# Eight of the first front's norms on GpSimd, the second power table's pools released tile by tile, all orders written anew

## The chip, the cores and the metric

The kernel runs on one core of one Trainium2 chip. The metric is the device time of a whole execution in microseconds (us). Three runs of the kernel before took 402.38, 403.27 and 403.44 us, median 403.27. PE is TensorE, PEld its weight load, DVE VectorE, ACT ScalarE, POOL GpSimd and SP SyncE; "L1108" is line 1108 of the kernel before.

## The reference

Four residual layers on `x` (1 x 2048 x 512, bf16): sliding attention A, state-space convolution B, and both again with the same weights. In A each of 32 heads (16 elements each) looks at 8 positions, two apart. B's convolution kernel `K` is a sum over 128 complex states, the same in both layers.

```python
def _A_ref(x, wqkv, wo):
    H = 32; Dh = D // H
    W, dil = 8, 2
    qkv = (x @ wqkv).reshape(B, S, 3, H, Dh).transpose(2, 0, 3, 1, 4)
    q, k, v = qkv[0], qkv[1], qkv[2]
    idx = pos[:, None] - (jnp.arange(W) * dil)[None, :]
    mask = idx >= 0
    logits = jnp.einsum("bhsd,bhswd->bhsw", q, k[:, :, idx_c, :]) * Dh ** -0.5
    attn = softmax(jnp.where(mask, logits, -1e9))
    o = jnp.einsum("bhsw,bhswd->bhsd", attn, v[:, :, idx_c, :])
    return o.transpose(0, 2, 1, 3).reshape(B, S, D) @ wo

def _B_ref(u, A_re, A_im, B_re, B_im, C_re, C_im, log_dt, Dskip):
    dt = jnp.exp(log_dt)[:, None]
    P = jnp.exp((dt * A)[:, :, None] * l[None, None, :])
    K = jnp.einsum("dn,dnl,dn->dl", Cc, P, dt * Bc).real
    y = irfft(rfft(pad(u, 2 * L)) * rfft(pad(K, 2 * L)))[:L]
    return y + u * Dskip

x = x + _A_ref(_layernorm(x), A_wqkv, A_wo)
x = x + _B_ref(_layernorm(x), A_re, A_im, B_re, B_im, C_re, C_im, log_dt, Dskip)
x = x + _A_ref(_layernorm(x), A_wqkv, A_wo)
x = x + _B_ref(_layernorm(x), A_re, A_im, B_re, B_im, C_re, C_im, log_dt, Dskip)
```

## The kernel before

`x` is held as 16 row tiles of 128 x 512, taken in four blocks of four. The kernel has five stages, and in each of them every engine takes its instructions in the order in which the program issues them; no scheduler reorders them. That order is written out by hand: a string with a letter or a word for each piece of work. The table gives the strings and roughly when the stage runs in the profiled execution.

| stage | string | us |
|---|---|---|
| first front, together with the making of `K` | `ORDERK`, read by `k_gen` (L995) | 0 to 110 |
| first attention core | `CORE0`, read by `LayerA.core` | 105 to 190 |
| first convolution and second front | `ORDER0`, `ORDERF` | 190 to 270 |
| second attention core | `CORE1` | 265 to 350 |
| second convolution | `ORDER1` | 350 to 401 |

*The first front and `K` (`ORDERK`).* `K` needs powers of a complex number for each channel and state. Eleven squarings make the powers with exponents 1, 2, 4 and so on: `s` squares on ACT (L1083), `i` is a doubled product and a difference on DVE (L1087, L1090). `b` copies each power into a table on ACT: `B_t` (L1099) or, for the powers from 8 to 128, `pow_t` (L1097), whose negated plane is another ACT copy (L1102) and whose repeated plane a DMA (`c`, L1105). `M` fills up `B_t` with products on DVE (L1108, through the scratch tile `cm_t`), seven groups, the last ones with the powers 256, 512 and 1024 as factors. `T` and `U` fill the second kind of table, `A_t`, in four chunks of 32: chunks 0 and 2 are `T` and stand in the pool `kg_tab0`, chunks 1 and 3 are `U` and stand in `kg_tab1`. `H` makes the heads of chunks 1 to 3 (L1225, an ACT copy). The first `H` calls `stage_two` (L1213), which closes the scratch pool `kg_small` and opens `kg_tab1` and `kg_out` on its room; these two wait until the whole of the old pool is released. `p` multiplies the tables on PE (L1266), `x` copies the products to `kgs` on ACT (L1274), and after the last letter `kgs` is stored (L1288). `G` are the steps that make the constant tables of the convolution: the mask products on POOL (L696) and, last of their kind, the store `w`.

Between these letters stands the first front. The layer norm of a row tile needs its sum and its sum of squares. For blocks 0 to 2 they are `a`, two passes on ACT for each row tile (L143, L1152); for block 3 `3`, one `bn_stats` on DVE. `l` are the small DVE operations that make the mean and the offset `ln_nb` (L1166, L1167, L1178), `W` makes the reciprocal deviation on ACT (L1184, L1185). `y` applies the norms of blocks 0 to 2, 12 on ACT (L193), and `z` those of block 3, 4 on DVE (L195). `t` transposes a block in two halves of eight 128 x 128 transposes (L1194), `e` copies each half to `xnT` on ACT (L1197), `k` and `q` project (L1204), `K` and `Q` copy the projections on ACT (L1209). `X` are the first three products of queries and keys (L340, `A_pr`, which take the room of `A_t` in `kg_tab0`), `Z` their sums on PE.

*The attention cores.* `m` multiplies queries and keys on DVE (L340), `l` sums on PE, `x`, `e`, `r`, `n` and `T` are the softmax. `P` multiplies weights and values on DVE (`pav`, L465), and `S` (half-width, L490) or `V` (whole-width, L480) sums on PE. `O` projects back and adds to `x`. `a` and `f` apply the norm of a row tile for the next layer on DVE and ACT. The core before the first convolution also holds the letters `A` to `H`, eight copies that bring `K` into `k_perm` (L1448); `KROWS` names the engine of each. `k_perm` and `g_i` also serve as scratch for an angle reduction on POOL (L728).

*The convolutions.* The transform of length 4096 is made of two steps. `K` and `U` are the first step for `K` and for the input, whose results are copied from PSUM into `a1s` (L788); `k` and `u` the second step, with copies to `kf_sb` and `ub` (L865); `m` is the product of the two spectra on DVE (L849, L852); `y` and `Y` are the first step of the inverse (half-width and whole-width on PE) with a copy to `z`; `z`, `w` and `v` the last step for different widths of columns, which adds to `x`. The second letter of a word names the engine of the copy or the addition: `A` is ACT, `D` is DVE.

*The second front (`ORDERF`).* `h` are the statistics of half rows, four `bn_stats` of 256 elements; `H` the same with whole rows of 512; `a` joins them; `p` makes the reciprocal deviation on ACT; `n` applies the norm of four row tiles, with `G` two on POOL and two on DVE and with `D` all four on DVE; `T` transposes, `E` copies the transposes, `P` and `Q` project.

Of the kernel before, what the change touches and what calls it, by code (L numbers as in the profile page):

```python
# [11 lines left out]
ALU = mybir.AluOpType  # L12
# [9 lines left out]
S = 2048  # L22
D = 512
H = 32
DH = 16
W = 8
NA = 16
NDT = 4
# [24 lines left out]
KD KA KA KA KD KA KD KA KD KA KD kA kD kA kA kD UA KD UA UD kA UA kD UA KD UA  # L53
UD UA KD kA u UD m UA KA u UD u UD m KA u kA m m UA u u kD m m u
UA u UD kA m UA kD kA u m kA kD u kA yA m YD m u m u YA u u m u
yA m m u yA m m YA yA yD yD
# [8 lines left out]
UA UD UA UD UA UA UD UA UD UA UD u UD u u UA m u m u m UA m u m u  # L65
UD m m UA u m u m u u yA YA u m m u yD m YA m u u m m u yA
YA m yA YD w000D yA yA yD yA z03D yA w010D yA yD yA z02D v103A v113D v112D v102D v110D v100A v111D v101A
"""

CORE0 = """  # L70
vvmvvlvmvvmlvxlemvrmnlqmqvlTvqlxevqmlvmvmPvvP1rnllxS0qTmqOeVmrqP4qSl2OPPSOSOPSmPP5On3l8ml6SPCOOV
AlxSPP7eOSrObSPn9POSdOESOPSPbDadBPfaGOtFOaaawVfHSbatO
"""
CORE1 = """
0m1l2ml3mvvqqlmmlmvqqvvllxmemqvlrnvvlmxTqqlvvmqlmvPvvvvmvqlleqVPrmxqmnqSTOePlPmSOPllSPOSPrOSnOPS
mOSPOblxOSPPdeOSrffbVPdfwOnPfVOPSOSPafbOPSdafftOSafatO
# [914 lines left out]
CH = 32  # L991
# [3 lines left out]
def k_gen(tc, nc, a_consts, ins, kd, la, x_v, lnst, zero, b_consts):  # L995

    B_L = (0, 1, 2, 3, 4, 5, 6, 7, 256, 258, 260, 262, 512, 516, 768, 772, 1024, 1280, 1536, 1792, 2048)
    NCH = P // CH
    with ExitStack() as ctx:
# [92 lines left out]
        def planes(k):  # L1092
            return cur[k][:].rearrange("p r (c x) -> p r c x", c=NCH)

        def power(k):
            if 3 <= k <= 7:
                nc.scalar.copy(Pw[:, :, k - 3, 1::2, :].rearrange("p c r x -> p r c x"), planes(k))  # L1097
            else:
                nc.scalar.copy(Bt[:, :, :, B_L.index(1 << k), :], cur[k][:].rearrange("p r (q g) -> p r q g", g=4))  # L1099

        def power_neg(k):
            nc.scalar.mul(Pw[:, :, k - 3, 2, :], planes(k)[:, 1], -1.0)  # L1102

        def power_copy(k):
            nc.sync.dma_start(Pw[:, :, k, 0, :], Pw[:, :, k, 1, :])  # L1105
# [48 lines left out]
        def norms():  # L1154
            D2 = D * D
            for b in range(4):
                cs = slice(4 * b, 4 * b + 4)
                rstd = la.fp.tile([P, 4], F32, name="ln_rstd")
                nb = la.fp.tile([P, 4], F32, name="ln_nb")
                ln[b] = rstd, nb  # L1160
                if b < 3:
                    mean, ms = lnst["s1"][:, cs], -1.0 / D
                    msq = la.fp.tile([P, 4], F32, name="ln_msq")
                    veps = la.fp.tile([P, 4], F32, name="ln_veps")
                    lvar[b] = veps[:]
                    yield lambda: nc.vector.scalar_tensor_tensor(msq[:], mean, -1.0 / D2, mean, ALU.mult, ALU.mult)  # L1166
                    yield lambda: nc.vector.scalar_tensor_tensor(veps[:], lnst["s2"][:, cs], 1.0 / D, msq[:], ALU.mult, ALU.add)  # L1167
                else:
                    ag = la.fp.tile([P, 4, 2], F32, name="ln_ag")
                    lvar[b] = ag[:, :, 1]  # L1170

                    def aggr():
                        for a in range(4):
                            nc.vector.bn_aggr(ag[:, a, :], lnst["bn"][:, 12 + a, 0, :])

                    yield aggr
                    mean, ms = ag[:, :, 0], -1.0
                yield lambda: nc.vector.scalar_tensor_tensor(nb[:], mean, ms, rstd[:], ALU.mult, ALU.mult)  # L1178
# [15 lines left out]
                    nc.tensor.transpose(pt[:, di, a, :], xb[b][:, a, (2 * d + di) * P:(2 * d + di + 1) * P], ident[:])  # L1194

        def turned(b, d):
            nc.scalar.copy(la.xnT[:, 2 * d:2 * d + 2, b * 512:(b + 1) * 512], xps[b, d][:].rearrange("p t a q -> p t (a q)"))  # L1197

        def proj(kind, b, ft, h):
            if h == 0:  # L1200
# [5 lines left out]

        def projected(kind, b, ft):
            dst = la.kT[:, ft, 14 + b * 4:18 + b * 4, :] if kind == "k" else la.qT[b][:, ft]
            nc.scalar.copy(dst.rearrange("p a q -> p (a q)"), pps[kind, b, ft][:])  # L1209
# [60 lines left out]
        def produced(c, q8):  # L1270
            if (c, q8) == (0, 0):
                late["kgs"] = late["kgp"].tile([P, NB * 4, P], BF16, name="kgs")
            q0 = c * CH + q8 * 8
            nc.scalar.copy(late["kgs"][:, :, q0:q0 + 8].rearrange("p m (h j) -> p m h j", h=2),  # L1274
                           pks[c, q8][:, :, 0:4 * NB * 4].rearrange("p h (j m) -> p m h j", j=4))

        def k_store():
# [44 lines left out]
        ops = dict(  # L1322
            s=calls(square, *((k,) for k in range(11))), i=[f for k in range(11) for f in calls(double, (k,)) + calls(differ, (k,))],
            b=[f for k in range(12) for f in calls(power, (k,)) + (calls(power_neg, (k,)) if 3 <= k <= 7 else [])],
            C=c_part(), M=b_part(), G=steps, w=[w2_store], c=calls(power_copy, *((k,) for k in range(5))),
            a=calls(pass_stats, *((b, a, i) for b in range(3) for a in range(4) for i in range(2))), l=norms(),
            W=calls(inv_std, *((b,) for b in range(4))), y=calls(apply, *((b, a, "act") for b in range(3) for a in range(4))),
            z=calls(apply, *((3, a, "dve") for a in range(4))),
            t=calls(turn, *((b, d) for b in range(4) for d in range(2))), e=calls(turned, *((b, d) for b in range(4) for d in range(2))),
            k=calls(proj, *(("k", b, ft, h) for b in range(4) for ft in fts for h in range(2))),  # L1330
            q=calls(proj, *(("q", b, ft, h) for b in range(2) for ft in fts for h in range(2))),
# [6 lines left out]
        ops["3"] = calls(lambda a: row_stats(nc, lnst, xb[3][:, a, :], 12 + a, "dve"), *((a,) for a in range(4)))  # L1338
# [240 lines left out]
```

## Time and profile before

The profiled execution took 402.72 us, 400.8 us of which is the span from its first to its last instruction; the median of the runs shown is 403.27. The granted TensorE clock was 0.999 of full speed. The table gives the busy time of each engine in seven stretches of the span, in us.

| stretch | PE | DVE | ACT | POOL |
|---|---|---|---|---|
| 0 to 10 | 3.16 | 6.15 | 7.37 | 9.17 |
| 10 to 100 | 44.30 | 89.27 | 82.35 | 12.46 |
| 100 to 180 | 73.25 | 79.77 | 57.81 | 32.06 |
| 180 to 270 | 81.55 | 83.16 | 80.85 | 11.43 |
| 270 to 350 | 76.59 | 79.08 | 56.18 | 1.02 |
| 350 to 380 | 25.29 | 28.41 | 28.51 | 0.00 |
| 380 to 400.8 | 15.88 | 15.65 | 12.94 | 0.00 |
| whole span | 320.0 | 381.5 | 326.0 | 66.1 |

A line of the groups reads: line of the code, engine, operation, output and inputs by the program's names, their shapes (partitions x elements) and types, the count; then the busy time of all, the mean of one in ns, and the idle time of the engine just before these instructions with what ended most of it. A line of the timeline gives the start of a run of like instructions, the time that they took together, the engine, the line and the operation; in brackets stands how long it waited and for what.

### The profile page before, as it was taken

What the parts mean: (1) busy time and instruction counts of PE and PEld (TensorE: products, weight loads), DVE (VectorE), ACT (ScalarE), POOL (GpSimd) and SP (SyncE); (2) the same over time, 40 slices, a digit from 0 to 9 for tenths busy, and PEclk for the clock granted to TensorE, in tenths of its full rate; (3) what the DMA queues carried; (4) which work ended last, traced back from release to release, by engine and by line L of the source; (5) the groups of instructions that cost most, each with busy time, mean ns of one, the idle gap of its engine ahead of it and who ended that gap; (6) DMA issues with size and microseconds to landing.
All of it is one profiled execution on the core that took longest, in us unless ns stands there. A gap on an engine that the chain in (4) does not pass through costs nothing.

```text
span 400.8 us, 14761 instructions
## 1 busy us (share of the span) xinstructions
PE 320.0 (80%) x6479; PEld 227.6 (57%) x6527; DVE 381.5 (95%) x475; ACT 326.0 (81%) x565; POOL 66.1 (17%) x79
## 2 busy tenths in 40 slices
PE   3000178789999899889997889999999998998795
PEld 2000037557635567656887878643456766667785
DVE  6999999999999999999999999979999999989995
ACT  7999999786656499888999998864655788989983
POOL 9402500000299600030500002300000001000000
PEclk9999999999999999999999999999999999999999
DMA  7942820323014855285235677740063009504606
GB/s 220 395 132 31 87 65 12 83 54 94 12 39 110 216 180 152 79 296 225 101 115 206 223 270 215 263 136 2 2 169 94 3 20 404 162 2 108 213 11 205
DMA packets 62322, 54.17 MB, mean 135 GB/s; under 512 B 33869, under 2 KB 50738, under 8 KB 60978
## 3 DMA queue, kind: packets, MB, share of 16 engines
q1 hardware_dynamic: 62250, 53.22, 43.6%
q8 instruction: 51, 0.84, 0.9%
q14 instruction: 13, 0.11, 0.1%
q10 hardware_dynamic: 8, 0.00, 0.0%
HBM read 30.15 MB, written 13.24 MB: 108 GB/s over the span
## 4 chain that ended last, share of the span: by engine, by line
PE 29%; DVE 21%; issue 9%; ACT 7%; DMA 4%; SPq 1%; POOL 0%; DVEq 0%; ACTq 0%
DVE pav L465 5%; PE pq L396 5%; PE pq L501 4%; PE po L490 4%; DVE prod L340 3%; PE pq L221 3%; DVE t L849 3%; DVE t L852 3%; DVE ln_bn L148 2%; PE pb L799 2%; DMA v_ext<-v_ext 2%; PE L L352 2%; DVE a1s L788 1%; PE pb L806 1%; PE pb L883 1%
## 5 line engine op out<-in xcount | busy, mean ns | idle before, releaser
L465 DVE TENSOR_TENSOR pav<-attn,v_ext 128x4096 bf16<-128x4096 bf16 (+1 forms) x34 | 72.6, 2169 | 0.2
L340 DVE TENSOR_TENSOR prod<-qT,kT_ext 128x4096 bf16<-128x4096 bf16 x29 | 66.6, 2322 | 0.4 <-ACT qT L223 0.3
L1108 DVE TENSOR_TENSOR A_t<-A_t,pow_t 128x1024 bf16<-128x1024 bf16 (+4 forms) x46 | 37.9, 870 | 0.2
L1194 PE MATMUL pt<-ident,x_blk 128*128 128x128 bf16 x64 | 6.3, 241 | 39.6 <-ACT x_blk L193 39.6
L501 PE MATMUL pq<-wop,oT 128*128 128x512 bf16 x122 | 31.7, 379 | 3.4 <-issue 2.5
L490 PEld LDWEIGHTS <-pav 64*128 64x128 bf16 x1664 | 26.0, 95 | 13.4 <-DVE pav L465 6.0
L490 PE MATMUL po<-ident,pav 64*128 64x64 bf16 x1664 | 29.0, 190 | 4.2 <-DVE pav L465 2.3
L865 ACT CAST ub<-pb 128x1024 bf16<-128x1024 f32 x32 | 31.9, 1068 | 0.2
L398 ACT CAST v_ext<-pq 128x512 bf16<-128x512 f32 x32 | 18.8, 586 | 16.1 <-PE pq L396 16.1
L1204 PE MATMUL pp<-xnT,kT_ext 128*128 128x512 bf16 x88 | 25.3, 404 | 7.8 <-ACT qT L1209 2.8
L806 PE MATMUL pb<-a1s,w_sb 128*128 128x64 bf16 x768 | 27.3, 193 | 5.0 <-ACT a1s L788 3.1
L396 PE MATMUL pq<-wv,xnT 128*128 128x512 bf16 x120 | 29.9, 379 | 0.4
L806 PEld LDWEIGHTS <-w_sb 128*128 128x128 bf16 x768 | 24.8, 98 | 7.2 <-issue 4.8
L1194 PEld LDWEIGHTS <-x_blk 128*128 128x128 bf16 x64 | 4.7, 107 | 42.0 <-ACT x_blk L193 40.4
L788 DVE CAST a1s<-pb 128x1024 bf16<-128x1024 f32 x21 | 24.7, 1214 | 2.5 <-PE pb L799 2.2
L788 ACT CAST a1s<-pb 128x1024 bf16<-128x1024 f32 x27 | 26.4, 1043 | 0.8 <-PE pb L799 0.8
L1266 PEld LDWEIGHTS <-A_t 128*64 128x64 bf16 (+1 forms) x512 | 21.9, 103 | 4.7 <-DVE A_t L1108 0.6
L1266 PE MATMUL pk<-B_t,A_t 128*64 128x84 bf16 (+1 forms) x512 | 23.7, 201 | 1.0 <-ACT kgs L1274 0.5
L221 PE MATMUL pq<-xnT,kT_ext 128*128 128x512 bf16 x92 | 23.0, 379 | 0.2
L176 POOL TENSOR_TENSOR ln_rstd<-ln_rstd,ln_mh 128x4 f32<-128x4 f32 x2 | 4.0, 2016 | 107.4 <-DVE ln_rstd L175 107.4
L396 PEld LDWEIGHTS <-xnT 128*128 128x128 bf16 x128 | 11.7, 97 | 14.3 <-issue 1.7
L492 ACT CAST oT<-po 128x512 bf16<-128x512 f32 x26 | 14.9, 575 | 5.8 <-PE po L490 5.8
(261 smaller groups left out, 902.9 us busy)
## 6 DMA issues: line engine op xcount, KB each, us to landing
w_sb<-w_dram SPq DMA_DIRECT2D x8, 1024.0 KB, 6.8
w_dram<-xnT SPq DMA_DIRECT2D x1, 4096.0 KB
kf_ring<-kf_dram SPq DMA_DIRECT2D x13, 256.0 KB, 4.5
kf_ring<-kf_dram SPq DMA_DIRECT2D x26, 128.0 KB, 3.9
v_ext<-v_ext SPq DMA_DIRECT2D x4, 784.0 KB, 6.4
x_blk<-in_A_x_dram SPq DMA_DIRECT2D x4, 512.0 KB, 4.7
kT_ext<-in_A_wqkv_dram SPq DMA_DIRECT2D x4, 512.0 KB, 9.5
x_sb<-in_A_x_dram SPq DMA_DIRECT2D x4, 512.0 KB, 6.1
```

Of the source, the lines that this page charges most:

```text
L221: nc.tensor.matmul(pq[:], lhsT=self.wqk[:, dt, ft * P:(ft + 1) * P], rhs=self.xnT[:, dt, q * 512:(q + 1) * 512], start=(dt == 0), stop=(dt ...
L340: nc.vector.tensor_tensor(pr, self.qT[q][:, ft].unsqueeze(1).to_broadcast([P, W, 4, P]), kap, ALU.mult)
L396: nc.tensor.matmul(pp[:], lhsT=xnT[:, dt, a * P:(a + 1) * P], rhs=wv[:, dt, :], start=(dt == 0), stop=(dt == NDT - 1))
L465: nc.vector.tensor_tensor(pv[:, i], attn[:, n % 4].unsqueeze(2).to_broadcast([P, W, DH // parts, H]), vap, ALU.mult)
L490: nc.tensor.matmul(po[:, h, 0, i * nt + ft, :], lhsT=pvf[rows, i, w, ft * P:(ft + 1) * P], rhs=ident[rows, rows], start=(w == 0 and ft + i ...
L501: nc.tensor.matmul(pw[:], lhsT=oT[:, ftp, :], rhs=self.wo[:, ftp, :], start=False, stop=(ftp == NDT - 1))
L788: (self.nc.scalar.copy if eng == "act" else self.nc.vector.tensor_copy)(dst, src)
L806: nc.tensor.matmul(p2[:, j, :], lhsT=self.w2[:, ec * EC + j, :], rhs=a1s[:, ec * EC + j, :], start=True, stop=True)
L865: nc.scalar.copy(ub[:], p2)
L1108: return lambda: nc.vector.tensor_tensor(*args)
L1204: nc.tensor.matmul(pps[kind, b, ft][:], lhsT=la.wqk[:, dt, c:c + P], rhs=la.xnT[:, dt, b * 512:(b + 1) * 512], start=(dt == 0), stop=(dt = ...
L1266: nc.tensor.matmul(o, lhsT=lhs, rhs=Bt[:, ri, c * CH + ql].rearrange("p b g -> p (b g)"), start=(not half and j % 4 == 0 and ri == 0), sto ...
```

## The change

*Engines by a table.* `ENGK` names an engine for each copy and norm of the first front. All copies stay on ACT. Of the 12 norms of blocks 0 to 2, five go to POOL and seven stay on ACT; of the four of block 3, two go to POOL, two to ACT, none to DVE. That makes 8 POOL norms, 8 ACT norms and no DVE norm, where there were 12 on ACT and 4 on DVE. `STATD` says which blocks take their statistics on DVE; it is block 3, as before.

*The release.* `kg_tab1` and `kg_out` get `reuse_waits="tile"`: a tile waits for the release of the old tiles whose room it takes, not of the whole old pool.

*The orders.* All six strings are new. In `ORDERK` the first `H` stands four letters behind the last `M`, where it stood eight behind; the first `U` comes eight letters behind that `H`, where it came two, and all `U` stand ahead of the first `X`, where three stood behind it. `KROWS` gives six of the eight `k_perm` copies to DVE, where there were three, and two to ACT, where there were five.

| what is counted | before | after |
|---|---|---|
| `CORE0`: norms for the convolution on DVE / ACT | 6 / 2 | 3 / 5 |
| `CORE0`: sums half-width / whole-width | 13 / 3 | 10 / 6 |
| first convolution: `a1s` copies of `K` on ACT / DVE | 8 / 8 | 11 / 5 |
| first convolution: copies of `K`'s spectrum on ACT / DVE | 10 / 6 | 8 / 8 |
| first convolution, inverse copies (`y`, `Y`, also in `ORDERF`) on ACT / DVE | 12 / 4 | 10 / 6 |
| second front: statistics of half rows / whole rows | 8 / 0 | 2 / 3 |
| second front: additions of four row tiles by 256 columns (`z`, two of them in `ORDER0` after) on ACT / DVE | 1 / 3 | 6 / 1 |
| second front: additions of 128 columns (`v`) on ACT / DVE | 8 / 0 | 1 / 1 |
| second front: copies of transposes on ACT / DVE | 4 / 4 | 2 / 6 |
| second front: norms on POOL / DVE | 6 / 10 | 8 / 8 |
| `CORE1`: norms for the convolution on DVE / ACT | 4 / 8 | 5 / 7 |
| `CORE1`: sums half-width / whole-width | 13 / 3 | 14 / 2 |

The diff, with the strings of the cores and of the convolutions and the plain renamings cut:

```diff
 ORDERK = """
-sCiibsCbiisCiiMbMCGMiMsabiMcbiasMbbCCaGiMMTsibGGTGTicMbGsbiaTbcisbbTTTMGiiTbTiMaGsaGGTMiGacMabTl
-MlMMMWMlaiMsiMayMwMiMybyaTMysteMMqatMaaMkeMadTkqMialKMMlQMkWMlaqMMcbqykTQHqUaUKqQaakUTyqUkyqUUpU
-KUkyUapxUxtaUpatpeUaldHQqeUqkKUkl3TT33TQkkxpWl3KxTpTxyxTylTWTpqlkyyTqpHKkzkQzxKUtkUktezUqqeUKTkT
-kQKztktkTeeKkUkUKTTkkKUUUkUxUUpxEUpkxpUkUUkpEKkKqxpkUxoxpEoKXqUokUkQUpKxpZxXxZXZ
+siCbCibCCisaGMiMiMsbMiCsiCGMibMcbsiibMbisiGTbcMbsTTGcMTiTTbGGabiTMsTbiaTbibcGTaiGsMMaaMiacTiMaba
+GGMMMlsMlTGiWaasMlMyTaiwTMyyaiaMayMtMeMtbkqlaMeMMTMMMkMqbKMqqMlMMQdaHqqQkaQaUWUalykUaKpqyyUakUyx
+qUQUkUptKUUatxaUeUplkpHqekUxTKTUkkKqpdTlQ3qTWxlkT3pxxyTyqyp3TkytQT3TlpKeqWTTqHUQktUkkelUkKzzTKkz
+UkkzkUTtEEKUUUTUxKeUktkUUUkKekUkpUxKkpkKxkxKEqUqokpokxpUQpkUUUKXxokpXxKpxXxZpZZx
 """
...
 ORDERF = """
-yA yA z01D yA z00D yA yD h00 yA h01 YA v100A v110A v102A v013A h10 a0 p0 n0G z02A v111A v101A S v112A
-h02 h11 T0 E00A a1 E01A z13D p1 n1G v003A P03 Q00 h12 a2 P01 T1 E10A p2 P00 E11D n2G h03 P11 P12
-P13 T2 E20A h13 a3 E21D P02 p3 n3D P22 P21 P10 T3 E30D E31D P23 P20 x1
+h00 v001A h10 z11A a0 p0 v011D n0G H1 S z13A a1 z02A z12A T0 E00D p1 n1G E01A z03A P02 H2 P01 T1
+a2 p2 E11D P03 E10A P00 n2G Q00 T2 P12 H3 E21D E20D P10 a3 p3 P11 P23 n3G P13 P22 T3 E30D x1
+P20 P21 E31D
 """
...
-KROWS = "ADDAADAA"
+ENGK = dict(b="AAAAAAAAAAAAAAAAA", y="AGAGGAGAGAAG", z="GGAA", e="AAAAAAAA", K="AAAAAAAAAAAAAAAA", Q="AAAAAAAA", x="AAAAAAAAAAAAAAAA")
+STATD = (3,)
+KROWS = "DDDDADDA"
...
+        def copy_by(eng):
+            return nc.scalar.copy if eng == "A" else nc.vector.tensor_copy
...
-            tab.append(ctx.enter_context(tc.tile_pool(name="kg_tab1", bufs=1)))
-            late["kgp"] = ctx.enter_context(tc.tile_pool(name="kg_out", bufs=1))
+            tab.append(ctx.enter_context(tc.tile_pool(name="kg_tab1", bufs=1, reuse_waits="tile")))
+            late["kgp"] = ctx.enter_context(tc.tile_pool(name="kg_out", bufs=1, reuse_waits="tile"))
...
-        fts = range(NDT)
+        fts, by = range(NDT), dict(A="act", D="dve", G="pool")
...
-            W=calls(inv_std, *((b,) for b in range(4))), y=calls(apply, *((b, a, "act") for b in range(3) for a in range(4))),
-            z=calls(apply, *((3, a, "dve") for a in range(4))),
+            W=calls(inv_std, *((b,) for b in range(4))), y=calls(apply, *((b, a, by[ENGK["y"][4 * b + a]]) for b in range(3) for a in range(4))),
+            z=calls(apply, *((3, a, by[ENGK["z"][a]]) for a in range(4))),
```

More of the change, by code (lines that the diff above doesn't have):

```diff
@@ L1160, in norms @@
                 ln[b] = rstd, nb
[L1161 removed]
+                if b not in STATD:
                     mean, ms = lnst["s1"][:, cs], -1.0 / D
@@ L1196, in turned @@
         def turned(b, d):
-            nc.scalar.copy(la.xnT[:, 2 * d:2 * d + 2, b * 512:(b + 1) * 512], xps[b, d][:].rearrange("p t a q -> p t (a q)"))
+            copy_by(ENGK["e"][2 * b + d])(la.xnT[:, 2 * d:2 * d + 2, b * 512:(b + 1) * 512], xps[b, d][:].rearrange("p t a q -> p t (a q)"))
         def proj(kind, b, ft, h):
@@ L1208, in projected @@
             dst = la.kT[:, ft, 14 + b * 4:18 + b * 4, :] if kind == "k" else la.qT[b][:, ft]
-            nc.scalar.copy(dst.rearrange("p a q -> p (a q)"), pps[kind, b, ft][:])
+            copy_by(ENGK["K" if kind == "k" else "Q"][4 * b + ft])(dst.rearrange("p a q -> p (a q)"), pps[kind, b, ft][:])
         At, At2, t2ts = {}, {}, {}
@@ L1273, in produced @@
             q0 = c * CH + q8 * 8
-            nc.scalar.copy(late["kgs"][:, :, q0:q0 + 8].rearrange("p m (h j) -> p m h j", h=2),
+            copy_by(ENGK["x"][c * CH // 8 + q8])(late["kgs"][:, :, q0:q0 + 8].rearrange("p m (h j) -> p m h j", h=2),
                            pks[c, q8][:, :, 0:4 * NB * 4].rearrange("p h (j m) -> p m h j", j=4))
@@ L1337, in k_gen @@
             x=calls(produced, *((c, j) for c in range(NCH) for j in range(CH // 8))), X=first_logits(), o=calls(lambda ft: la.front_ext(3, "act", ft), (0,), (1,), (2,)), Z=calls(lsum, (0,), (1,), (2,)))
-        ops["3"] = calls(lambda a: row_stats(nc, lnst, xb[3][:, a, :], 12 + a, "dve"), *((a,) for a in range(4)))
+        ops["3"] = calls(lambda b, a: row_stats(nc, lnst, xb[b][:, a, :], 4 * b + a, "dve"), *((b, a) for b in STATD for a in range(4)))
         ops = {key: iter(v) for key, v in ops.items()}
```

38 lines of the change are left out of this document (21 added, 17 removed).

## The prediction

> **What bounds the kernel now.** I read the page first: busy time by engine, then the 40 slices.
>
> ```profile
> PE 320.0 (80%) x6479; PEld 227.6 (57%) x6527; DVE 381.5 (95%) x475; ACT 326.0 (81%) x565; POOL 66.1 (17%) x79
> ...
> DVE  6999999999999999999999999979999999989995
> ACT  7999999786656499888999998864655788989983
> POOL 9402500000299600030500002300000001000000
> ```
>
> VectorE (DVE) is the bound: only 400.8 - 381.5 = 19.3 us of the span lie outside it. POOL stands empty from slice 6 to 10 (50 to 107 us), where the change puts it to work. Next, the sums by stretch, to see where those 19.3 us are (columns: stretch, length, busy time of PE, PEld, DVE, ACT, POOL, clock, DMA).
>
> ```profile
> 100.00:180.00 80.00, 73.25 (x1430) 46.23 (x1443) 79.77 (x52) 57.81 (x114) 32.06 (x17) 1.00 0.46 134
> 180.00:190.00 10.00, 8.76 (x190) 6.15 (x194) 9.53 (x21) 8.81 (x19) 0.00 (x0) 1.00 0.59 229
> 190.00:236.00 46.00, 40.14 (x1217) 37.16 (x1216) 43.50 (x59) 45.26 (x52) 6.04 (x8) 1.00 0.47 169
> 236.00:270.00 34.00, 32.65 (x499) 23.30 (x503) 30.12 (x79) 26.78 (x45) 5.38 (x7) 1.00 0.69 226
> ```
>
> From 100 to 180 us DVE idles 0.23 us, from 180 to 270 us 0.47 + 2.50 + 3.88 = 6.85 us. In the ten-microsecond stretches it also idles 3.85 us at the start, 1.6 us from 350 to 360 and 5.3 us after 380; from 10 to 100 us under 1 us in all. So the first stage, where the eight norms are, has no gap to fill: whatever DVE loses or saves there moves the end one for one. Third, the groups by form, for prices (last figures: busy us, mean ns of one).
>
> ```profile
> L195 DVE TENSOR_SCALAR x_blk<-x_blk,ln_rstd,ln_nb 128x512 bf16<-128x512 bf16 x4 | 1.5, 407 | 0.0
> L193 ACT ACTIVATE x_blk<-x_blk,ln_nb,ln_rstd 128x512 bf16<-128x512 bf16 x12 | 9.4, 804 | 0.3 <-DVE ln_nb L1178 0.3
> L195 POOL TENSOR_SCALAR xnT<-x_sb,ln_rstd,ln_nb 128x512 bf16<-128x512 bf16 x8 | 6.0, 771 | 17.0 <-DVE ln_nb L183 17.0
> L728 POOL TENSOR_SCALAR k_perm<-k_perm,aux 128x512 int32<-128x512 int32 x4 | 16.4, 4098 | 0.0
> ```
>
> The eight norms that POOL does at 190 us cost it 771 ns each; there DVE copies from PSUM. L728, also 128x512, takes 689 ns at its fastest and 4098 ns on average while DVE multiplies two SBUF tensors. So POOL is slow beside such products. The timeline of DVE in that window shows that DVE pays as well.
>
> ```profile
> 118.08 4.51 DVE L340 TENSOR_TENSOR prod<-qT,kT_ext 128x4096 bf16<-128x4096 bf16 x2
> 122.51 1.09 DVE L443 TENSOR_TENSOR ex<-ex,rs 128x1024 bf16<-128x1024 bf16 x1
> ...
> 126.86 7.09 DVE L340 TENSOR_TENSOR prod<-qT,kT_ext 128x4096 bf16<-128x4096 bf16 x3
> 133.88 4.89 DVE L465 TENSOR_TENSOR pav<-attn,v_ext 128x4096 bf16<-128x4096 bf16 x2
> ```
>
> Undisturbed, two such products took 4.48 us (104.8 us), so three take 6.72 and a 128x1024 one 0.68. The excess is 0.03, 0.41, 0.37 and 0.41 us here, and 0.70 us in three products at 109.6 us (7.42): 1.92 us for the eight L728 of the window, **0.24 us of DVE per POOL instruction**. A second price: the four mask products of L696 (37.2 to 45.2 us) cost DVE only three small operations of 0.26 instead of 0.15 us, 0.08 each.
>
> **The change part by part.**
>
> *DVE's own work*, counted from both kernels' instruction lists. First front: four norms leave, -1.5. Copies of `k_perm`: three more, 3 x 0.41 = +1.2. Norms into `xnT` in the first core: three fewer at 5.0/13 = 0.385, -1.15. First convolution and second front: copies into `a1s` -3 x 1.18 = -3.5; K-spectrum copies +2 x 1.22 = +2.4; inverse copies +2 x 1.22 = +2.4; residual adds from three wide ones to one and a half, -1.8; row statistics 32 x 0.34 = 10.9 become 8 x 0.34 + 12 x 0.68 = 10.9, 0; norms -2 x 0.4 = -0.8; copies of transposes +2 x 0.65 = +1.3; together 0.0. Second core: one norm, +0.4. Last convolution: one copy +1.2, adds -1.2. Sum **-1.05 us**.
>
> *ACT* loses about 6.8 us by the same count (first front -4 x 0.78, `k_perm` -3 x 1.03, the rest smaller). In the first front this hides under DVE. From 190 to 236 us, where ACT is busy 45.26 of 46, its copies before the last spectral product go from 48 to 50; what is gained is at the end of that stage, where DVE gets the copies instead. I price ACT at nothing. PE has 144 matmuls fewer (more whole-width sums); it idles 5.9 us from 190 to 236 us, so nothing again.
>
> *POOL's eight norms against DVE.* In stage one DVE runs products of two SBUF tensors nearly without a break. By L728, 8 x 0.24 = +1.92. Lower bound by the masks, 8 x 0.08 = 0.66; upper bound 8 x 0.771 = 6.2, if DVE stands still for all of each norm. I take 1.92: it has the same shape and operation; the masks write 64 elements on half the lanes.
>
> The Trainium skill (SBUF — State Buffer, Who interferes with whom) says that a DVE instruction with two SBUF inputs and a GpSimd instruction that reads SBUF exclude each other, the later one waiting until the other is done. The trace agrees that both wait (4098 ns, 0.24 us), but DVE's measured loss is a third of the whole 0.7 to 0.77 us; by the rule alone the term would be the 6.2 us above. It speaks against this change.
>
> *POOL's norms as a new wait.* Rows 1 and 3 of block 0 now stand on POOL behind the masks.
>
> ```profile
> 37.16 2.89 POOL L696 TENSOR_TENSOR Wp<-s_Wp,aux 64x64 bf16<-64x64 f32 x2 [22.44 <-ACT s_Wp L677]
> 40.11 5.11 POOL L696 TENSOR_TENSOR WpJ<-s_WpJ,aux 64x64 bf16<-64x64 f32 x2
> ...
> 48.70 0.99 ACT L1197 COPY xnT<-pt 128x1024 bf16<-128x1024 bf16 x1
> ```
>
> Ahead of the masks' sine ACT now has three more row sums (0.62 each) and one more `B_t` copy (0.94): 2.8 us later, so POOL is free at 48.0. `ln_nb` is there at 45.7 (42.94, and 2.7 us more DVE work ahead of it). The first norm meets the 4096-wide product that now stands at about 47.8 to 50.0 and ends at 50.8; the second waits out one 0.6 us product: 52.1. Eight transposes and the hand-over, 0.75: 52.85. ACT, in order, comes to the copy `xnT<-pt` at 50.4 and waits; behind it stands the cast that makes `B_t` 1024 (0.95 + 0.95). DVE multiplies by it at 54.5 (50.46 before; now a 4096 product, a 2048 add and one `differ` more ahead: +4.1). The copy must start by 52.6, so the stall is 0.25, **+0.3**. Bounds: none at 0.77 per norm; 4.4 at 4.1 per norm. Blocks 1 to 3 have more room: block 1's `ln_nb` falls at about 63, the ACT copy that needs its transposes at 69; block 3's norms end at 87 to 90 instead of 85.9, but the first logits product, at 100.8 before, now stands behind all table work, at about 103.
>
> *Second table by tile, among the last B products.* DVE comes to its first product at 60.25 without a gap and ACT copied its head at 58.74 without waiting for the release: nothing to win. In the new order the head copy stands at about 57 on ACT and its user at about 62 on DVE; the 5 us between cover it, and the `w2` stores that it waits for ended at 48.3. Zero; if ACT is late by the 4.4 above, still zero.
>
> *Second front, block 3 on POOL.* Before, four DVE norms of 1.38 us, then 0.85 us of waiting for transposes. Now two POOL norms (847 each) end 1.7 us after `ln_nb`, DVE's two after 0.8, so DVE waits about 1.7 us: +0.85. Nothing covers the rstd of block 3 any more, +0.15; that of block 0 is now covered by a 0.62 us add, -0.51. **+0.5**, between 0 and 1.2.
>
> *All other orders* move work between neighbours; in the cores DVE has no gap to win or (by the list) to lose: 0, bounds -3.4 (half of the 6.85 us) and +2.
>
> Sum: -1.05 + 1.92 + 0.3 + 0.5 = +1.7. The profiled execution took 402.72 us, 400.8 of it span: 404.4. The median of the runs shown is 0.55 higher: **404.9 us**. I call 0.3% (1.2 us) the least difference that can be told from none.
>
> **Rivals.**
>
> *The new orders fill the gaps of the first convolution and second front* (faster). For it: 6.85 us of idle time in 90 us, ACT with less to do, better shared inverse copies (11 on ACT and DVE as 8 and 3 become 9 as 5 and 4). Against: the copies and products to be done are as many, and the chain statistics, rstd, norm, transpose, projection is as long as before. If half the idle time goes (-3.4), POOL costs 0.08 a norm (+0.66) and nothing else: -3.8, 398.9, by the median 399.5. It decides once the gaps shrink by more than 1.7 + 1.2 = 2.9 us.
>
> *No change that can be told*: the gaps shrink by about what POOL costs, 1.7: 403.3.
>
> *POOL and DVE exclude each other entirely*: 6.2 for 1.92, 409.2.
>
> *Block 0 late*: 4.1 us a norm as in L728, the stall 4.4 for 0.3: 409.0; it decides from a second norm that ends after 51.9 on.
>
> *The tile-wise release does nothing*: as argued; no time of its own.
>
> **Chances.** Forecast 0.38 (its own range 404.5 to 407), filled gaps 0.36, no change 0.17, exclusion 0.04, late block 0.05. Slower by over 0.3%: 0.38 + 0.04 + 0.05 = 0.47; within: 0.17; faster: 0.36. The range reaches down to 399.0, for most of the filled gaps, and up to 408.5, for a norm's cost of 0.41 (the worst single excess, 8 x 0.41 = 3.3) with 2 us of stall: 399.0 to 408.5.
>
> **What would show it.** Right: POOL's `x_blk` norms last 1.5 to 3 us, DVE products beside them are longer by 0.2 to 0.4, and the first logits product starts 0.5 to 1.5 us later than its DVE work alone says. Wrong: POOL norms near 0.8 us and products at 0.60 steps (the 1.92 falls); an idle DVE at 54 us of several microseconds (the stall was too small); idle from 180 to 270 us under 4 us (the gaps were filled after all).

## The result and the profile after

Four runs of the changed kernel took 407.61 to 409.44 us, median 408.4; four of the kernel before beside them 402.38 to 403.44, median 402.97. The ratio is 1.0137, 95% interval 1.0109 to 1.0166: the change costs 5.4 us. Its profiled execution took 408.68 us with a span of 406.9. Line numbers are two higher than before up to `k_gen` and nine higher from its products on (L1108 is L1117 now). The page's busy times and slices:

```profile
PE 321.7 (79%) x6336; PEld 229.5 (56%) x6383; DVE 379.9 (93%) x461; ACT 319.6 (79%) x555; POOL 69.5 (17%) x89
...
DVE  6999959999999899999999998979999999989994
ACT  7999949788646569997999996755655867999982
POOL 9300941042089000100500001310000001000000
```

DVE has 1.6 us less to do and 7.7 us more idle time (406.9 - 379.9 = 27.0 against 19.3). The sixth slice (51 to 61 us), full before on both, is at 5 on DVE and at 4 on ACT. The stretches of the prediction, in the same columns:

```profile
100.00:180.00 80.00, 75.52 (x1275) 49.23 (x1290) 77.20 (x53) 57.09 (x109) 19.75 (x17) 1.00 0.46 125
180.00:190.00 10.00, 8.33 (x190) 5.71 (x192) 9.07 (x12) 7.32 (x21) 0.00 (x0) 1.00 0.80 329
190.00:236.00 46.00, 41.11 (x1256) 37.14 (x1250) 45.12 (x65) 45.47 (x55) 6.06 (x8) 1.00 0.49 173
236.00:270.00 34.00, 31.24 (x521) 23.84 (x520) 29.45 (x66) 25.66 (x39) 7.05 (x9) 1.00 0.71 216
```

From 100 to 180 us DVE now idles 2.80 us, not 0.23. The groups that answer to the prices:

```profile
L197 POOL TENSOR_SCALAR x_blk<-x_blk,ln_rstd,ln_nb 128x512 bf16<-128x512 bf16 x8 | 10.9, 1375 | 29.3 <-PE pk L1275 12.4 <-DVE ln_nb L1187 11.2 <-DVE A_t L1117 5.6
L698 POOL TENSOR_TENSOR WpJ<-s_WpJ,aux 64x64 bf16<-64x64 f32 x2 | 10.2, 5104 | 0.1
L730 POOL TENSOR_SCALAR k_perm<-k_perm,aux 128x512 int32<-128x512 int32 x4 | 7.4, 1864 | 0.0
```

The norms on POOL last 1375 ns in the mean; the second pair of masks takes twice what it took (10.2 for 5.1 us). To see where the 6.1 us of span are, the timelines of DVE are cut at points that both kernels have:

| DVE from the point before up to | before | after | difference | idle before, after |
|---|---|---|---|---|
| end of the last `A_pr` product (from 0) | 109.30 | 112.88 | +3.6 | 4.6, 8.4 |
| first copy into `a1s` (first core) | 79.47 | 81.65 | +2.2 | 0.7, 3.7 |
| end of the last spectral product | 47.93 | 46.01 | -1.9 | 2.5, 0.9 |
| first product of the second core | 32.42 | 33.95 | +1.5 | 3.9, 5.8 |
| first copy into `a1s` (second core) | 87.85 | 87.51 | -0.3 | 2.5, 2.1 |
| end of the last spectral product | 27.43 | 27.44 | 0 | 0, 0 |
| end of the span | 16.44 | 17.45 | +1.0 | 5.2, 6.1 |

The first stage loses most, all of it as idle time of DVE (8.4 for 4.6 us). POOL and DVE there (start, length):

```profile
41.50 1.66 POOL L698 TENSOR_TENSOR Wp<-s_Wp,aux 64x64 bf16<-64x64 f32 x2 [27.66 <-ACT s_Wp L679]
43.21 10.27 POOL L698 TENSOR_TENSOR WpJ<-s_WpJ,aux 64x64 bf16<-64x64 f32 x2
53.59 1.92 POOL L197 TENSOR_SCALAR x_blk<-x_blk,ln_rstd,ln_nb 128x512 bf16<-128x512 bf16 x2
...
```

```profile
45.35 0.41 DVE L1117 TENSOR_TENSOR B_t<-B_t,cm_t 128x512 bf16<-128x512 bf16 x1
...
52.63 0.68 DVE L1117 TENSOR_TENSOR B_t<-B_t,cm_t 128x1024 bf16<-128x1024 bf16 x1
53.23 0.26 DVE L1175 SCALAR_TENSOR_TENSOR ln_msq<-ln_s 128x4 f32<-128x4 f32 x1
53.42 0.68 DVE L1117 TENSOR_TENSOR B_t<-B_t,cm_t 128x1024 bf16<-128x1024 bf16 x1
58.30 0.70 DVE L1117 TENSOR_TENSOR B_t<-B_t 128x1024 bf16<-128x1024 bf16 x1 [4.20 <-ACT B_t L1105]
```

In the kernel before DVE came to the same product without a wait:

```profile
50.46 0.68 DVE L1108 TENSOR_TENSOR B_t<-B_t 128x1024 bf16<-128x1024 bf16 x1
```

The fourth mask runs from 45.46 to 53.48 us, 8.02 us (1.99 before). All that time DVE multiplies without a break, and the mask ends with `ln_msq`, the first small operation. The two norms then take 1.16 and 0.77 us. Who waits for them, on PE and ACT:

```profile
54.80 0.40 PE L1203 MATMUL pt<-ident,x_blk 128*128 128x128 bf16 x2 [7.20 <-POOL x_blk L197]
```

```profile
56.31 1.01 ACT L1206 COPY xnT<-pt 128x1024 bf16<-128x1024 bf16 x1 [5.61 <-PE pt L1203]
57.22 1.05 ACT L1105 CAST B_t<-sq_z 128x1024 bf16<-128x1024 f32 x1
```

The profile's spans on POOL are rough, but PE's wait of 7.20 us ends with the first norm too. ACT waits 5.61 us for the transposes, the cast of the power 1024 stands behind their copy, and DVE waits 4.20 us for the cast.

Two things said ahead of the prediction have to be put right here, since the argument rests on POOL's order. The mask products are no steps of `ORDERK`: the program issues them by the letter `m` of `LATE0`, in the first convolution, long after the norms. And the order is not held by hand on every engine in every stage: behind the first stage `manual_schedule` names PE, DVE, ACT and SP (`MAN`), not POOL. POOL ran the masks at 41 us, ahead of norms that the program issues earlier; the scheduler placed them there, and no letter of a string shows it.

### The profile page after: what moved, and what is told of

Read it like the earlier page. It is cut to its first block, busy times and chain, and to the rows that moved or that the text cites. A ratio compares the mean times of both kernels' runs of the same rounds, so it can differ in the third digit from the quotient of the medians.

```text
span 406.9 us, 14464 instructions
## 1 busy us (share of the span) xinstructions
PE 321.7 (79%) x6336; PEld 229.5 (56%) x6383; DVE 379.9 (93%) x461; ACT 319.6 (79%) x555; POOL 69.5 (17%) x89
## 4 chain that ended last, share of the span: by engine, by line
PE 36%; DVE 21%; issue 8%; ACT 7%; DMA 2%; SPq 2%; POOL 0%; DVEq 0%; ACTq 0%; POOLq 0%
DVE pav L467 7%; PE pq L398 5%; PE pq L223 3%; DVE prod L342 3%; PE po L492 3%; DVE a1s L790 3%; PE pk L1275 3%; PE pq L503 2%; PE pp L282 2%; PE L L350 2%; DVE t L854 2%; PE pp L1213 1%; PE pb L881 1%; PE pb L801 1%; PE L L354 1%
## 5 line engine op out<-in xcount | busy, mean ns | idle before, releaser
L467 DVE TENSOR_TENSOR pav<-attn,v_ext 128x4096 bf16<-128x4096 bf16 (+1 forms) x34 | 72.2, 2160 | 1.7 <-ACT v_ext L400 1.2
L342 DVE TENSOR_TENSOR prod<-qT,kT_ext 128x4096 bf16<-128x4096 bf16 x29 | 65.7, 2298 | 1.3 <-PE L L350 0.7
L1117 DVE TENSOR_TENSOR A_t<-A_t,pow_t 128x1024 bf16<-128x1024 bf16 (+4 forms) x46 | 39.2, 897 | 0.2
L400 ACT CAST v_ext<-pq 128x512 bf16<-128x512 f32 x32 | 18.8, 587 | 16.4 <-PE pq L398 16.4
L492 PEld LDWEIGHTS <-pav 64*128 64x128 bf16 x1536 | 24.0, 95 | 11.4 <-issue 5.4
L808 PE MATMUL pb<-a1s,w_sb 128*128 128x64 bf16 x768 | 26.4, 193 | 4.3 <-ACT a1s L790 1.5
L790 ACT CAST a1s<-pb 128x1024 bf16<-128x1024 f32 x30 | 28.8, 1057 | 0.8 <-PE pb L801 0.8
L492 PE MATMUL po<-ident,pav 64*128 64x64 bf16 x1536 | 26.8, 190 | 2.6 <-issue 1.4
L790 DVE CAST a1s<-pb 128x1024 bf16<-128x1024 f32 x18 | 21.3, 1217 | 1.9 <-PE pb L801 1.8
L509 ACT ACTIVATE x_sb<-pq 128x512 bf16<-128x512 f32 x24 | 14.3, 596 | 9.7 <-PE pq L503 9.7
L225 ACT CAST qT<-pq 128x512 bf16<-128x512 f32 x24 | 14.1, 587 | 8.2 <-PE pq L223 7.1
L178 POOL TENSOR_TENSOR ln_rstd<-ln_rstd,ln_mh 128x4 f32<-128x4 f32 x2 | 2.1, 1034 | 106.2 <-DVE ln_rstd L177 106.2
```

What stands on the lines that cost most here:

```text
L342: nc.vector.tensor_tensor(pr, self.qT[q][:, ft].unsqueeze(1).to_broadcast([P, W, 4, P]), kap, ALU.mult)
L467: nc.vector.tensor_tensor(pv[:, i], attn[:, n % 4].unsqueeze(2).to_broadcast([P, W, DH // parts, H]), vap, ALU.mult)
L492: nc.tensor.matmul(po[:, h, 0, i * nt + ft, :], lhsT=pvf[rows, i, w, ft * P:(ft + 1) * P], rhs=ident[rows, rows], start=(w == 0 and ft + i ...
L790: (self.nc.scalar.copy if eng == "act" else self.nc.vector.tensor_copy)(dst, src)
L808: nc.tensor.matmul(p2[:, j, :], lhsT=self.w2[:, ec * EC + j, :], rhs=a1s[:, ec * EC + j, :], start=True, stop=True)
L1117: return lambda: nc.vector.tensor_tensor(*args)
```

## The experiments

Stage lengths are those of the table above, from one profiled execution each. In some executions the granted clock drops for a stretch (0.91 from 110 to 150 us in the run with the masks behind, 0.95 from 240 to 275 us in that with the new convolution's order alone, 0.93 from 170 to 195 us in that with the first stage back); lengths from those stretches are not used. In several runs it is also 0.83 to 0.87 from 60 to 70 us, where DVE waits for PE in none of them.

| run | median, before beside it | ratio, interval |
|---|---|---|
| block 0's norms on ACT | 405.31, 403.58 | 1.0069, 1.0038 to 1.0099 |
| all norms back | 407.39, 403.58 | 1.0096, 1.0073 to 1.0119 |
| small operations among the products | 407.81, 403.58 | 1.0117, 1.0083 to 1.0151 |
| masks behind the norms | 409.83, 403.58 | 1.0154, 1.0121 to 1.0187 |
| the eight norms alone | 407.39, 403.27 | 1.0114, 1.0092 to 1.0136 |
| first core's order alone | 403.11, 403.27 | 1.0007, 0.9982 to 1.0032 |
| first convolution, second front alone | 403.74, 403.27 | 1.0031, 1.0002 to 1.0061 |
| second core, second convolution alone | 403.40, 403.27 | 1.0000, 0.9987 to 1.0012 |
| first stage back | 403.36, 403.34 | 1.0003, 0.9989 to 1.0017 |
| four late norms alone | 405.30, 403.34 | 1.0052, 1.0033 to 1.0071 |
| release back | 412.70, 403.34 | 1.0227, 1.0204 to 1.0250 |
| blocks 0 and 3 off POOL | 404.34, 403.34 | 1.0017, 1.0003 to 1.0031 |

**Block 0's norms on ACT.**

```diff
-ENGK = dict(..., y="AGAGGAGAGAAG", ...)
+ENGK = dict(..., y="AAAAGAGAGAAG", ...)
```

> The changed kernel with the four norms of block 0 on ACT again (six POOL norms left). Theory 'mask queue': the 4.20 us for which DVE waits at 54.1 us come from block 0's two POOL norms standing behind the fourth mask; then that wait falls under 0.5 us, ACT gets 1.6 us more, and the time falls by 3.5 to 4.2 us, to 404.2 to 404.9 us. Rival 'POOL against DVE': each POOL norm costs DVE the same wherever it stands; then two norms fewer give back a quarter of the 5.4 us, and the time is about 407. Rival 'orders': DVE waits for B_t because the new order brings ACT to that cast too late; then the wait stays above 3 us and the time within 1 us of 408.4.

```profile
54.86 0.69 DVE L1117 TENSOR_TENSOR B_t<-B_t 128x1024 bf16<-128x1024 bf16 x1 [0.79 <-ACT B_t L1105]
```

The wait falls from 4.20 to 0.79 us, the first stage is 2.9 us shorter (109.98), and the ratio falls by 0.7%, 2.7 us. That is the theory's mechanism at less than its size: the wait stays above the 0.5 us expected, and the time above 404.9. A loss spread evenly over the eight norms would have given back 1.4.

**All norms back.**

```diff
-ENGK = dict(..., y="AGAGGAGAGAAG", z="GGAA", ...)
+ENGK = dict(..., y="AAAAAAAAAAAA", z="DDDD", ...)
```

> The changed kernel with all norms of the first front where they were (12 on ACT, 4 on DVE); orders and release as changed. Theory 'mask queue': the wait of 4.2 us goes, DVE gets 1.5 us of norms back and is rid of what the other six POOL norms cost it (1.3 us more in the table products than before); the time is 404 to 404.8, so 1 to 2 us above the kernel before, which is what the new orders cost by themselves. Rival 'POOL against DVE': all that was lost was lost to POOL's norms, and the time is 403 or under. Rival 'orders': at 407 or above.

By its time this is the rival "orders" (407 or above), though block 0's wait falls to 0.79 us. DVE now waits 1.72 us for ACT at 85.7 and 0.51 at 77 us, and the table work ends at 111.51, later than with six norms on POOL. With 12 norms ACT comes late in this order. So the new order loses with the old engines too, and what it costs apart from the engines can't be read from this run.

**Small operations among the products.**

```diff
+        js = sp.tile([P, 4], F32, name="js")
+        ops["j"] = calls(lambda n: nc.vector.scalar_tensor_tensor(js[:], lnst["mh"][:], -1.0, lnst["mh"][:], ALU.mult, ALU.mult), *((n,) for n in range(4)))
-...MyTaiwTMyyaia...
+...MyTjaijwTjMjyyaia...
```

> The changed kernel with four added DVE operations of 128x4 f32 that nothing uses, among the products that DVE runs from 45.7 to 54.1 us. Theory 'starved': POOL's mask products end when DVE comes to a small operation, not between products; the fourth mask then ends at the first of them, at about 47 us instead of 53.5, the two norms behind it end before 52, the wait at 54 us falls under 1 us, and the time falls by 3 to 4 us to 404.4 to 405.4 although DVE has 0.4 to 1 us more to do. Rival 'slow mask': the fourth mask takes 8 us for a reason of its own (its data, its place); then nothing moves but DVE's 0.4 to 1 us, and the time is 408.8 to 409.4.

```profile
43.20 3.85 POOL L695 TENSOR_TENSOR WpJ<-s_WpJ,aux 64x64 bf16<-64x64 f32 x2
47.15 8.20 POOL L194 TENSOR_SCALAR x_blk<-x_blk,ln_rstd,ln_nb 128x512 bf16<-128x512 bf16 x2
```

```profile
46.80 0.26 DVE L1346 SCALAR_TENSOR_TENSOR js<-ln_mh 128x4 f32<-128x4 f32 x1
...
47.59 0.15 DVE L1346 SCALAR_TENSOR_TENSOR js<-ln_mh 128x4 f32<-128x4 f32 x1
...
49.86 0.15 DVE L1346 SCALAR_TENSOR_TENSOR js<-ln_mh 128x4 f32<-128x4 f32 x1
...
50.54 0.57 DVE L1346 SCALAR_TENSOR_TENSOR js<-ln_mh 128x4 f32<-128x4 f32 x1
```

(Its line numbers are three lower.) Half of the theory holds. The fourth mask takes 1.60 us and ends with the first added operation, at 47.04; so its 8 us were set by DVE's products and not by the mask. But the norms behind it now meet the same products: 3.95 and 4.26 us. The first passed two small operations (0.15 us each, not lengthened) and got in at the fourth (0.57); the second got in when DVE had run dry. DVE still waits 3.36 us, and the time stays: 407.81, neither theory's size.

**Masks behind the norms.**

```diff
+                if c == "y" and ny == 4:
+                    C["masks"]()
...
-    late["m"] = C["masks"]
+    late["m"] = lambda: None
```

> The changed kernel with the mask products (and the clearing of their tiles) behind block 0's two norms on POOL instead of ahead of them. Theory 'mask queue': the norms start at ln_nb, 45.4 us; if they get in between products as those of block 3 did (2.3 and 3.0 us each), they end by 51, the wait at 54 us is under 1 us, and the time is 404.2 to 405.4. Rival 'norms starve too': a norm has to wait for a small DVE operation just as the mask did; the first one then ends at 53.5 and the second after it, the wait stays at 3 us or more and the time at 407.5 to 408.4.

```profile
45.17 9.78 POOL L197 TENSOR_SCALAR x_blk<-x_blk,ln_rstd,ln_nb 128x512 bf16<-128x512 bf16 x2 [31.37 <-DVE ln_nb L1187]
...
55.17 0.64 POOL L698 TENSOR_TENSOR Wp<-s_Wp,aux 64x64 bf16<-64x64 f32 x2
```

The rival, with a time above its bounds. The first norm starts at `ln_nb` and lasts 9.02 us, until DVE stands still; it passed a small operation at 52.9 us, so it did not wait for one as the rival said. The second then takes 0.77 and a mask 0.29. DVE waits 4.1 us as in the changed kernel. The masks ahead of the norms are not the cause: in this order the first thing that POOL has to do from 45 us on, mask or norm, waits for the end of DVE's run.

**The eight norms alone**, in the order before.

```diff
-y=calls(apply, *((b, a, "act") ...)), z=calls(apply, *((3, a, "dve") ...)),
+y=calls(apply, *((b, a, dict(A="act", G="pool")["AGAGGAGAGAAG"[4 * b + a]]) ...)), z=calls(apply, *((3, a, dict(A="act", G="pool")["GGAA"[a]]) ...)),
```

> The kernel before with the eight norms on POOL and nothing else changed (old orders, old release; the other eight norms on ACT). Theory 'starved': the masks end at 45.2 as before, the two norms of block 0 start there and get in between products at 2.3 to 3 us each, so they end at 49.8 to 51.2; ACT's copy of the transposes, at 48.7 before, comes 2 to 3 us later and DVE waits 0 to 2 us; DVE saves 1.5 us of norms and pays about 1.3 us in its products: 402.5 to 405. Rival 'POOL against DVE': as much slower as the whole change, 406 to 409. Rival 'no cost': POOL's norms only take work off DVE and ACT, and the time is 401.5 to 402.

The rival's size. Block 0's and 1's norms take 2.15, 2.76, 4.35 and 3.17 us. DVE has 1.63 us of norms less, but its table products are 3.2 us longer, 0.40 for each POOL norm, and it waits 1.5 us more; the first stage ends at 112.92.

**Four late norms alone**, in the order before.

```diff
-y=calls(apply, *((b, a, "act") ...)), z=calls(apply, *((3, a, "dve") ...)),
+y=calls(apply, *((b, a, dict(A="act", G="pool")["AAAAAAAAGAAG"[4 * b + a]]) ...)), z=calls(apply, *((3, a, dict(A="act", G="pool")["GGAA"[a]]) ...)),
```

> The kernel before with four POOL norms alone: rows 0 and 3 of block 2 and rows 0 and 1 of block 3, which in the run with all eight ended in 0.77 to 1.18 us each; rows 2 and 3 of block 3 go to ACT. Theory 'place decides': DVE saves 1.5 us of norms, pays 0 to 0.4 us, nothing waits for the POOL norms, and the table work ends 0.8 to 1.5 us earlier than in the kernel before: 401.7 to 402.5. Rival 'POOL against DVE': each POOL norm costs DVE 0.45 us as in the run with all eight in the old order (3.7 us over 8); then DVE saves nothing, and the time is 403 to 404.

```profile
77.42 1.94 POOL L195 TENSOR_SCALAR x_blk<-x_blk,ln_rstd,ln_nb 128x512 bf16<-128x512 bf16 x2 [32.20 <-DVE ln_nb L1178]
```

```profile
77.68 1.12 DVE L1108 TENSOR_TENSOR A_t<-A_t,pow_t 128x512 bf16<-128x512 bf16 x2
78.83 0.80 DVE L1108 TENSOR_TENSOR A_t<-A_t,A_t 128x512 bf16<-128x512 bf16 x1
```

The rival's mechanism, with a time above its 404, though these norms take only 0.77 to 1.18 us. In the kernel before the same products took 0.75 and 0.42: each norm makes one of them 0.38 us longer. Four norms off DVE save 1.63, four on POOL make the table products 1.52 us longer. Of the 1.5 us that the first stage is longer, 1.1 are idle time: ACT's two norms of block 3 come late, PE waits 1.2 us for them, and DVE 0.87 us for a copy into `kT_ext` at 102 us.

**First core's order alone; first convolution and second front alone; second core and second convolution alone.** Each is the kernel before with the strings (and for the first `KROWS`) of the changed one.

> The kernel before with the order of the first attention core and the engines of its eight copies as changed. In the changed kernel the stretch from the last table work to the first copy into a1s is 2.2 us longer, with DVE waits of 0.71, 0.53, 1.16 and 0.48 us for PE and ACT. Theory 'order of the core': the waits are its own, and the time is 404.5 to 405.5. Rival 'inherited': the waits come from the first stage, which leaves PE and ACT late; then this kernel is within 0.8 us of the one before.

> The kernel before with the orders of the first convolution and second front as changed. In the changed kernel the convolution is 1.9 us shorter up to its last spectral product and the second front 1.5 us longer. Theory 'each stage by itself': -0.4 us, 402.2 to 403.0. Rival: the gain in the convolution was only the room that the late first stage had left (a late start hidden again), and this kernel is 1 us or more slower than the one before.

> The kernel before with the orders of the second attention core and the second convolution as changed. In the changed kernel the core is 0.3 us shorter and the convolution, up to the last store, 1.1 us longer. Theory 'each stage by itself': +0.7 us, 403.3 to 404.2. Rival: the end is set by stores that come late for another reason, and the time is within 0.3 us of the kernel before.

By themselves the later orders do nothing that these times can tell, or next to nothing. The first run is the rival's. The middle one has the widest interval, 0 to 0.6%, and its 403.74 lies between the theory and its rival. In the first run's profile the core is 0.7 us longer, and not 2.2, and DVE's three waits in the core's first 30 us (0.71, 0.53 and 1.16 us in the changed kernel) are not there; so these come from the first stage. The first convolution behind it, in its old order, is 1.7 us shorter (46.21), nearly the changed kernel's gain in the convolution without the convolution's new order. Of the third run the rival's size came out, with no sign of its cause.

**First stage back.**

The kernel before with `KROWS`, `CORE0`, `ORDER0`, `ORDERF`, `CORE1` and `ORDER1` as changed; `ORDERK`, the engines of the norms and the release of the whole pool are those of before.

> The changed kernel with the whole first stage as before (order, engines of the norms, release), all other orders as changed. Theory 'first stage': the loss was made in the first stage, by the wait behind the masks and by an order that leaves PE and ACT late for the first core; then the first core is 0.7 us longer than before and not 2.2, the first convolution 1.7 to 1.9 us shorter, the rest within 1 us, and the time is 402.0 to 403.3, at or just under the kernel before. Rival 'all orders cost': the later orders lose by themselves, and the time is 404.5 or above.

403.36 against 403.34: the whole loss is the first stage's or follows from it. The five other orders together bring nothing. The three early waits of the core are absent here too. The lengths that the theory gave can't be checked: core and convolution (1.5 and 0.3 us longer than before in this profile, 0.7 and -1.8 expected) reach into its stretch of low clock.

**Release back.**

```diff
-... tc.tile_pool(name="kg_tab1", bufs=1, reuse_waits="tile") ...
+... tc.tile_pool(name="kg_tab1", bufs=1) ...
```

(and the same for `kg_out`)

> The changed kernel with kg_tab1 and kg_out waiting for the release of the whole old pool again. Theory of the prediction: the release does nothing, since the head's copy on ACT (62.9 us) and its first user on DVE (66.1 us) come well behind the last use of the scratch pool; then the first stage has the same length within 0.3 us and the time is 407.5 to 409. Rival: the head now stands so close behind the last B products that a release of the whole pool would hold up ACT; then the table work ends 0.5 to 2 us later and the time is 409 or above.

```profile
66.29 0.40 ACT L1234 COPY A_t<-c_t 128x256 bf16<-128x256 bf16 x1 [3.36 <-issue]
```

The rival, and more: 412.7. ACT's head copy waits 3.36 us, to 66.29, when DVE has just ended its last product through `cm_t` (64.84 + 1.29 = 66.13), and the reciprocal deviation behind it on ACT makes DVE wait 2.04 us. In the changed kernel the head is copied at 62.86.

**Blocks 0 and 3 off POOL.**

```diff
-ENGK = dict(..., y="AGAGGAGAGAAG", z="GGAA", ...)
+ENGK = dict(..., y="AAAAGAGAGAAG", z="DDAA", ...)
```

> The changed kernel with block 0's norms on ACT and block 3's first two norms on DVE instead of POOL (four POOL norms left, in blocks 1 and 2). In the run with only block 0 on ACT, block 3's two POOL norms took 2.3 and 3.0 us and PE waited 1.36 us for the second; the first core stayed 2.2 us longer than in the kernel before, with DVE waiting for PE and ACT. Theory 'POOL holds up PE': that wait leaves PE behind at the start of the first core; without it the core is 1.0 to 1.4 us shorter, DVE's work is the same (two norms more, two delays of 0.38 fewer), and the time is 403.7 to 404.5. Rival 'order': PE is behind because all table work now stands ahead of the first logits; the core stays within 0.4 us of 81.66 and the time is 405 to 405.7.

In the run with block 0 on ACT these two lines stand on PE and POOL (the changed kernel has them three microseconds later):

```profile
90.89 0.56 PE L1203 MATMUL pt<-ident,x_blk 128*128 128x128 bf16 x7 [1.36 <-POOL x_blk L197]
```

```profile
85.53 5.31 POOL L197 TENSOR_SCALAR x_blk<-x_blk,ln_rstd,ln_nb 128x512 bf16<-128x512 bf16 x2 [6.03 <-DVE A_t L1117]
```

With the two on DVE, PE's wait is gone, the first stage as long (110.01), and the first core 80.90 for 81.66: 0.8 us, against the 1.0 to 1.4 expected. The time lies within the theory's bounds, 404.34. DVE's first wait in the core shows what block 3 has to do with it, with block 0 alone on ACT and in this run:

```profile
115.48 2.56 DVE L342 TENSOR_TENSOR prod<-qT,kT_ext 128x4096 bf16<-128x4096 bf16 x1 [0.72 <-PE L L350]
```

```profile
115.16 2.37 DVE L342 TENSOR_TENSOR prod<-qT,kT_ext 128x4096 bf16<-128x4096 bf16 x1 [0.24 <-PE L L350]
```

It is 0.71 or 0.72 us in all five profiles of the changed order with block 3's first two norms on POOL, 0.24 and 0.16 in the two with them on DVE. But the next wait, for ACT, grows from 0.54 to 0.77 us, and the largest part of the 0.8 us is another wait, 0.83 us for `v_ext` at 136 us. It is absent here, but also in the run with the small operations, where block 3 stood on POOL (core 80.50), and it is 1.32 us with all norms back. So 0.2 to 0.5 us of the core's length are shown to be block 3's, and why `v_ext` comes late in some runs is open.

With the norms of blocks 0 and 3 off POOL the ratio falls from 1.0137 to 1.0017, so in this order nearly the whole loss came in by these four norms. What is left over the kernel before is 0.17%, 0.7 us. No run was faster than the kernel before by more than its interval.

## Why the prediction was right, and where it was off

It forecast 404.9 us, slower, between 399.0 and 408.5. The time came out at 408.4: the direction was right, the size three times too small, and the range just held it. That it held was luck: its upper end stood for 3.3 us of POOL's norms against DVE with 2 us of stall, where 1.6 and 4.2 were measured.

*The wait behind block 0's norms* was there as described, link by link (masks, norms, transposes, ACT's copy, the cast of 1024, DVE's product), and its size was the error: +0.3 us forecast, 4.20 measured. The step that failed is "POOL is free at 48.0": it moved the four masks by 2.8 us and kept their lengths. They began 4.3 us later (41.50 for 37.16) and took 12.0 us for 8.1. The last one had taken 1.99 us because DVE came to a small operation or a gap so soon; at its new place 7.8 us of products stand behind `ln_nb`, and it took 8.02. A POOL instruction's length was taken for its own property; here it was set by what DVE ran beside it, and the new order of DVE showed that run. The rival "block 0 late" had the price, 4.4 of stall, but by norms of 4.1 us each; the run with the masks behind shows the same wait with a norm of 9.0 us in the mask's place. Its condition, a second norm that ends after 51.9, was met at 55.5, and 0.05 was too little for it.

*POOL's norms against DVE*: 1.92 forecast. The table products (`A_t` by `pow_t`, and the sums) are 1.25 + 0.33 = 1.6 us longer than before. The term held in size, not quite in its making: it is not 0.24 for each norm but, by the two runs in the old order, 0.38 to 0.40 us for one that gets in between two products, and nothing for one that meets an idle DVE (with block 0 on ACT the products are still 1.6 us longer). Of the forecast signs the longer products came; norms of 1.5 to 3 us did not, but for the last two (2.28 and 3.05; the others 0.77 to 1.18).

The Trainium skill (SBUF — State Buffer, Who interferes with whom) has the two exclude each other for a whole instruction. On POOL's side the traces agree and go further: POOL waited not for one DVE instruction but through nine (8.02 us). On DVE's side they don't: about 0.38 us, half of the norm's 0.77. The rival made from that rule, 6.2 us for the term, is out: DVE's products lost 1.6.

*Filled gaps*, the rival with 0.36, is out as well: from 180 to 270 us DVE idles 0.93 + 0.88 + 4.55 = 6.36 us, where it was 6.85.

*Blocks 1 to 3 have more room*: right for DVE, which never waited for them in the first stage, and wrong for PE. Block 3's norms took 2.28 and 3.05 us and ended at 93.7, not by 90 (at 90.8 where block 0 was on ACT, so most of the delay is block 0's); PE waited 1.49 us for them. By the waits in the core 0.2 to 0.5 of its 2.2 us are shown to follow from that.

*All other orders: 0.* Right as a sum (1.0003). That the cores have nothing to lose is not borne out: the first lost 0.7 us by its own order in that order's profile, and the convolution behind it was 1.7 shorter. That DVE's wait in the core leaves work done on the others would explain it, but no run shows this.

*Second front: +0.5.* The changed kernel shows +1.5 there, with the forecast wait for block 3's transposes (1.50 us against 0.85 before, forecast 1.7), but also 1.49 us for an addition on ACT that was not forecast. In runs with the same order it is +0.1 to +1.0 (32.54 to 33.37). With the convolution ahead of it giving and taking, this term stays unsettled.

*The release: zero.* As a sum it was: DVE reaches the first product of the second table without a gap in both kernels. But in the new order it carries 0.9%, 3.6 us (1.0227 against 1.0137); "nothing to win" was argued from the old order, where no run tried it, and the 5 us of cover forecast for the new order were 3.2 (head copied at 62.86, used at 66.08).

*DVE's own work, -1.05*: with the 1.92 the forecast was +0.9, measured -1.6. About half of the difference, 1.3 us, is in the products of the two cores (65.7 for 66.6, 72.2 for 72.6). POOL's L730, which runs beside those of the first core, took 7.4 for 16.4 us; that the two belong together was not tested.

*What was to show it wrong* did: "an idle DVE at 54 us of several microseconds". One reading was a little off: after 380 us DVE idled 5.2 us, not 5.3; nothing hangs on it.

## What to carry to other kernels

Beside VectorE's products of two SBUF tensors, run back to back, GpSimd was no free engine here: a norm moved off VectorE saved 0.41 us there and cost 0.38. Before an instruction is put on GpSimd, look in the order at the run of products that will stand beside it, not at the instruction's mean duration; what hangs on it can be as late as that run is long (9.02 us here). Look also at what really stands ahead of it on GpSimd: the masks were there by no letter of the order. A part that does nothing by itself can be what another part needs: undo each in the changed kernel too, not only alone in the old one.

## What the hardware showed

A mask product of 64x64 takes 0.29 us beside an idle DVE, 0.73 to 3.06 in most places and 8.02 at worst. Of the nine mask products looked at, eight ended within 0.03 us of the end of a small DVE operation (128x4 f32), which was then 0.26 us long instead of 0.15. Norms of 128x512 followed another rule: they passed four such operations without getting in, and got in at a later boundary, between two products or, once, at a small operation; those of blocks 0 and 1 in the old order did so after 1.6 to 3.7 us. From there they took 0.53 to 0.61 us, and the DVE instruction that began with them lasted 0.27 to 0.47 us longer, mostly 0.38 to 0.42. Which boundary lets POOL in was not settled.
